# Staging the output sums of a four-pass MLP in contiguous scratch and reordering its seven block products

## The chip, the cores and the metric

The kernel runs on one core of a Trainium2 chip as one program. The metric is the device time of that program in microseconds (us); several executions are timed and their median is given. One execution is also recorded by the hardware profiler, and all rows below come from it. The engines are called PE (TensorE, matrix products; PEld is its weight load), ACT (ScalarE), DVE (VectorE), POOL (GpSimd) and SP (SyncE, which here only issues transfers). L1302 is line 1302 of the kernel file.

## What is computed

Three layers follow one another: an attention with random features, a mixture of experts in which each of 2304 tokens goes through one of 8 experts, and a dense MLP. The change touches the MLP alone:

```python
def _moe2_ref(x, w_in, w_out):          # x 2304x512, w_in 512x2048, w_out 2048x512
    h = x @ w_in
    g = np.where(h >= 1, h, np.where(h <= -1, 0.0, (h + 1) ** 2 / 4))
    return (g @ w_out).astype(np.float32)
```

Inside the kernel the tokens stand sorted by expert, so a finished row of the output has to be written to the row of its token.

## The kernel before, in words

Attention and experts end near 399 us of the trace; the MLP fills the rest. Every float32 factor is split in a high and a low part, and a product is three matrix products: high by high, high by low, low by high.

**Passes and groups.** The 2048 hidden columns are taken in four passes `qd` of 512 columns (four blocks `f` of 128). The 2304 tokens are six groups `g` of G = 384 (three tiles `t` of 128). For each pass and group a hidden step makes g, and an output step `z_o(qd, g, fs)` multiplies it with 512 rows of w_out: 36 matmuls of 512 columns, half of them for blocks 0 and 1, half for blocks 2 and 3, into three PSUM banks `po`, one for each tile. Each output is thus a sum over four passes.

**Output sums before.** After the second half of `z_o`, ACT copies each bank to a tile `tmp` of 512 columns (L1298), and `z_store` (L1302) lets POOL issue an indirect transfer that scatters the 128 rows to the output tensor in DRAM: a plain write in pass 0, an accumulating one in passes 1 to 3. That is 15 tiles times 4 passes. The last group's three tiles (`ends`) are summed on chip in `acc` and written once at the end.

**The ring `tmp`.** `temp()` (L1236) hands out four buffers in turn. Three users share them: these copies, the four block combinations of `y_sums` (pass 0), and the four temporaries of `s_h` (s1, u2, s5, u3). A buffer that fed a transfer comes free when the transfer has landed.

**Pass 0** uses plain products, `z_h` (24 matmuls of 384 columns for two blocks). In between, POOL forms sums of blocks of the input (`y_sums`, L1312), ACT and DVE split them, and SP writes them to scratch `yd` in DRAM.

**Passes 1 to 3** take pairs `p` of token groups and halves `a` of the hidden blocks by Strassen's scheme in Winograd's form: `s_h(qd, p, a)` needs seven products instead of eight. Each product is six matmuls of 384 columns. They go to four PSUM banks b1 to b4, and ACT and DVE add the banks up to four results q11, q12, q21, q22, each followed by `z_clip` and `z_g` (clip, square, maximum, split). Each `s_h` is followed by the output step of one group, so a pass is six half steps, each an `s_h` and a `z_o`. The seven factors of the tokens come from `yd` through a ring of nine slots `yS`/`ys`; POOL issues a load (`y_load`, L1329, 768 KB) each time a product with a = 1 has read its slot.

**Order on the engines.** Every engine works through its instructions in program order. Between the output step and the next `s_h` stand calls of `w_advance`, which turn raw weights into float32 (`w_float32`: ACT L248, DVE L249 to L252) and split them. For each pass, two of these calls end in `w_sums` (L308), which forms the block sums of the weights: copies on ACT (L290), sums and low parts on POOL (L317 to L323, L293). The sums for passes 2 and 3 stand right before `s_h(qd, 0, 1)` and `s_h(qd, 1, 1)` of passes 1 and 2; those for pass 1 stand in pass 0.

At the end of the program a branch looks whether any expert had more tokens than its place holds (here none), and then the three tiles of `acc` are stored.

Of the kernel before, what the change touches and what calls it, by code (L numbers as in the profile page):

```python
# [8 lines left out]
F32 = mybir.dt.float32  # L9
# [4 lines left out]
AF = mybir.ActivationFunctionType  # L14
# [5 lines left out]
P = 128  # L20
# [141 lines left out]
def kernel(  # L162
# [145 lines left out]
    def w_sums(qd, sub, a, b):  # L308
        if sub == 0:
            for i in range(7):  # L310
                w_new(("wi", qd, "A", i))
        a11, a21 = [a.rearrange("p (a i f) -> p i a f", a=2, i=2)[:, i] for i in range(2)]
        a12, a22 = [b.rearrange("p (a i f) -> p i a f", a=2, i=2)[:, i] for i in range(2)]
        w_op(qd, 0, sub, a11)
        w_op(qd, 2, sub, a22)
        s1, s2, s3, s4 = a22, a11, a21, a22
        nc.gpsimd.tensor_add(s1, a21, a22)  # L317
        nc.gpsimd.tensor_sub(s3, a11, a21)
        nc.gpsimd.tensor_sub(s2, s1, a11)
        w_op(qd, 1, sub, s2)  # L320
        w_op(qd, 3, sub, s1)
        w_op(qd, 4, sub, s3)
        nc.gpsimd.tensor_sub(s4, a12, s2)  # L323
        for i, t in ((5, a12), (6, s4)):
            if qd == 1:
                w_op(qd, i, sub, t)
            else:
                wlast.append((qd, i, sub, t))
# [907 lines left out]
    def temp():  # L1236
        return zp.tile([P, 512], F32, name="tmp", tag="tmp", bufs=4)

# [61 lines left out]

    def z_store(t, src, op=ALU.bypass):
        nc.gpsimd.indirect_dma_start(  # L1302
            out=outs[t], out_offset=bass.IndirectOffsetOnAxis(ap=oidx[:, t:t + 1], axis=0),
            in_=src, in_offset=None, compute_op=op)


    def y_keep(u):
        p, i = divmod(u, 2)
        for j, op in (((0, 0), (1, 5)) if i == 0 else ((1, 6),)):
            nc.sync.dma_start(out=yd[p][op], in_=ys[u % 2][:, j * 4 * G:j * 4 * G + 4 * G].bitcast(F32))  # L1310

    def y_sums(p, s):  # L1312
        b11, b12, b21, b22 = [yT[2 * i + s][:, (2 * p + j) * G:(2 * p + j) * G + G] for i in range(2) for j in range(2)]
        t1, t2, t3, t4 = [temp()[:, 0:G] for _ in range(4)]
# [4 lines left out]
        for i, (op, t) in enumerate(((3, t1), (4, t3), (1, t2), (2, t4))):  # L1319
            tag = "g0" if i % 2 else "g1"  # L1320
# [11 lines left out]
    def s_h(qd, p, a):  # L1332
        k0 = 7 * (3 * (qd - 1) + p)
        b1, b2, b4, b3 = [ps_h2.tile([P, 512], F32, name="ph2", tag="ph2")[:, 0:G] for _ in range(4)]

        def product(i, bank, first, final):
            y = yslots[(k0 + i) % NSL].rearrange("p (s h c) -> p s h c", s=2, h=2)
# [8 lines left out]

        s1, u2, s5, u3 = [temp()[:, 0:G] for _ in range(4)]
# [21 lines left out]
        q12 = z_clip(u2)  # L1369
        z_g(*q22, (qd, g1, f1), nc.vector)  # L1370
        z_g(*q12, (qd, g1, f0), nc.vector)


# [51 lines left out]
    tot = nc.values_load(ints[0:1, 3, 0:1], min_val=0, max_val=8 * 16)  # L1425
    yT = y_tiles("yF")
    fw = [yT[j // 10][:, j % 10 * 256:j % 10 * 256 + 256] for j in range(16)]
# [8 lines left out]
    with tc.If(tot > 0):  # L1436
        for t in ends:
            nc.sync.dma_start(out=sd[t * P:(t + 1) * P, :], in_=acc[t])
        nc.sync.dma_start(out=ld.rearrange("(t p) o -> p t o", p=P), in_=oidx.rearrange("p (t o) -> p t o", o=1))
        for e in range(E):  # L1440
# [4 lines left out]
            with tc.For_i(0, cnt_e, 1) as i:  # L1445
# [54 lines left out]
                nc.sync.dma_start(out=sd[bass.ds(c0, 128), :], in_=fo)  # L1500
        for t in ends:
            nc.sync.dma_start(out=acc[t], in_=sd[t * P:(t + 1) * P, :])
    for t in ends:
        z_store(t, acc[t])

# [30 lines left out]
```

## Time and profile before

| | us |
|---|---|
| median of 3 runs | 948.33 |
| lowest and highest | 945.34, 952.28 |
| the profiled execution | 952.49 |
| its span in the trace | 950.7 |
| PE busy in it | 794.0 |
| MLP, from the first to the last matmul | 399.4 to 938.5 |

A profiled row gives an instruction's start, its duration, engine, line and operands. Square brackets at its end give how long the engine had stood idle before it, and which instruction or transfer ended that idleness. The granted clock of TensorE is shown as a share of full speed.

### The profile page before, as it was taken

To read this page: it belongs to the slowest core of one execution; us is meant where nothing else is said; L and a number is where in the kernel's file an instruction comes from. 1 tells how busy PE (TensorE), PEld (TensorE's weight loads), DVE (VectorE), ACT (ScalarE), POOL (GpSimd) and SP (SyncE) were. 2 spreads that over 40 slices of the span, in tenths; PEclk is the share of its full clock that TensorE was granted. 3 is DMA by queue.
4 is the path that set the end of the run, shared out by engine and by line. 5 is a ranking of instruction groups with operands and counts; after the bars stand their busy time and mean duration, and the time that the engine had idled before them with its cause. 6 is when DMAs were issued, how large, how long until landed. Compare 5 with 4: busy or idle time off the path is not lost. (4 is left out here: it accounts for less than half of the span.)

```text
span 950.7 us, 17112 instructions
## 1 busy us (share of the span) xinstructions
PE 794.0 (84%) x6428; PEld 715.9 (75%) x6428; DVE 541.1 (57%) x1097; ACT 412.3 (43%) x999; POOL 500.7 (53%) x527
## 2 busy tenths in 40 slices
PE   6897996899999999966587885968877779898984
PEld 5786885699999999955466774858666668787873
DVE  4578788566668565773554545444464444553441
ACT  6897995333222222343444443333333333443340
POOL 5468814455554552666555736463546464564333
PEclk9999998899999999987889997979988989998998
DMA  9956112556676655452445765584927484854723
GB/s 221 236 125 175 36 36 90 159 177 198 203 214 195 198 181 171 157 182 89 176 155 189 269 262 211 126 267 100 299 55 272 94 276 73 243 216 75 208 33 70
DMA packets 97260, 159.53 MB, mean 168 GB/s; under 512 B 28864, under 2 KB 61760, under 8 KB 97168
## 3 DMA queue, kind: packets, MB, share of 16 engines
q1 hardware_dynamic: 77408, 84.47, 29.8%
q0 software_dynamic: 18864, 72.16, 25.8%
q10 hardware_dynamic: 896, 1.70, 0.5%
q8 instruction: 53, 0.87, 0.4%
q14 instruction: 39, 0.32, 0.1%
HBM read 120.57 MB, written 37.75 MB: 167 GB/s over the span
## 5 line engine op out<-in xcount | busy, mean ns | idle before, releaser
L1286 PE MATMUL po<-wh,g 128*128 128x512 f32 x288 | 120.8, 419 | 40.0 <-ACT g L1249 23.4
L1250 POOL TENSOR_TENSOR g<-cl,g 128x384 fp32r<-128x384 f32 x60 | 65.6, 1101 | 156.8 <-ACT g L1249 121.3
L272 POOL TENSOR_SCALAR wh<-wraw 128x1024 fp32r<-128x1024 f32 x60 | 74.2, 1238 | 102.4 <-DMA wraw<-in_moe_w_dram 60.8
L1288 PE MATMUL po<-wh,g 128*128 128x512 f32 x288 | 120.7, 419 | 3.2 <-POOL g L1250 3.1
L1302 POOL DMA_INDIRECT out_dram<-tmp,oidx x60 | 88.0, 1467 | 60.0 <-ACT tmp L1298 47.6
L1287 PE MATMUL po<-wl,g 128*128 128x512 f32 x288 | 119.1, 414 | 0.0
L1286 PEld LDWEIGHTS po<-wh,g 128*128 128x128 f32 x288 | 57.9, 201 | 55.2 <-ACT g L1249 26.0
L1242 ACT ACTIVATE cl<-cl,half 128x384 f32<-128x384 f32 x96 | 56.1, 612 | 91.7 <-DVE cl L1241 91.7
L340 DVE TENSOR_TENSOR wl<-wraw,wh 128x1024 fp32r<-128x1024 f32 x60 | 86.9, 1456 | 9.8 <-POOL wh L272 9.8
L570 ACT ACTIVATE pp<-ps,bi 128x128 f32<-128x128 f32 x288 | 84.5, 480 | 3.1 <-DVE bi L566 3.1
L1341 PE MATMUL ph<-yS,wh 128*128 128x384 f32 x140 | 52.0, 372 | 37.4 <-DVE tmp L1352 31.8
L1110 PE MATMUL ph<-xh,wh 128*128 128x288 f32 (+6 forms) x256 | 77.6, 303 | 2.7 <-DVE hl L1116 2.2
L1128 PE MATMUL py<-hh,wh 128*128 128x288 f32 (+6 forms) x256 | 77.5, 303 | 0.0
L1111 PE MATMUL ph<-xl,wh 128*128 128x288 f32 (+6 forms) x256 | 77.2, 302 | 0.1
L1112 PE MATMUL ph<-xh,wl 128*128 128x288 f32 (+6 forms) x256 | 77.1, 301 | 0.0
L1130 PE MATMUL py<-hh,wl 128*128 128x288 f32 (+6 forms) x256 | 76.4, 299 | 0.0
L1129 PE MATMUL py<-hl,wh 128*128 128x288 f32 (+6 forms) x256 | 76.3, 298 | 0.0
L1288 PEld LDWEIGHTS po<-wh,g 128*128 128x128 f32 x288 | 57.7, 200 | 23.0 <-POOL g L1250 9.5
L1249 ACT ACTIVATE g<-cl 128x384 fp32r<-128x384 f32 x96 | 50.2, 525 | 46.7 <-DVE cl L1248 43.5
L1341 PE MATMUL ph<-ys,wh 128*128 128x384 f32 x112 | 43.1, 385 | 30.0 <-DVE tmp L1352 27.7
L1287 PEld LDWEIGHTS po<-wl,g 128*128 128x128 f32 x288 | 57.9, 201 | 12.6
L293 POOL TENSOR_TENSOR wl<-wz,wh 128x256 fp32r<-128x256 f32 (+1 forms) x54 | 49.3, 1019 | 28.2 <-ACT wh L290 27.9
(208 smaller groups left out, 2096.4 us busy)
## 6 DMA issues: line engine op xcount, KB each, us to landing
wraw<-in_moe_w_dram SPq DMA_DIRECT2D x57, 512.0 KB, 4.0
yS<-yd POOLq DMA_DIRECT2D x35, 768.0 KB, 9.4
ys<-yd POOLq DMA_DIRECT2D x28, 768.0 KB, 9.0
yd<-g SPq DMA_DIRECT2D x24, 384.0 KB, 2.6
wraw<-in_moe_w_in_dram SPq DMA_DIRECT2D x16, 512.0 KB, 4.7
wraw<-in_moe_w_out_dram SPq DMA_DIRECT2D x16, 512.0 KB, 4.3
yd<-ys SPq DMA_DIRECT2D x9, 768.0 KB, 7.1
blk<-in_k_dram SPq DMA_DIRECT2D x8, 512.0 KB, 7.1
```

Of the source, the lines that this page charges most:

```text
L340: nc.vector.tensor_sub(lo, t, hi.bitcast(F32))
L570: act.activation(at(ppb)[:, 2 * j + i, :], at(pjb[i])[:, j, :], AF.Exp, bias=r["bi"][:, j, i:i + 1])
L1110: nc.tensor.matmul(ph, lhsT=wh[:, d, c], rhs=xh, start=(d == 0), stop=False)
L1111: nc.tensor.matmul(ph, lhsT=wh[:, d, c], rhs=xl, start=False, stop=False)
L1112: nc.tensor.matmul(ph, lhsT=wl[:, d, c], rhs=xh, start=False, stop=(d == 3))
L1128: nc.tensor.matmul(py, lhsT=wh[:, a, c], rhs=hh, start=(f == 0), stop=False)
L1130: nc.tensor.matmul(py, lhsT=wl[:, a, c], rhs=hh, start=False, stop=(f == 7))
L1286: nc.tensor.matmul(po, lhsT=gh[:, c], rhs=wh, start=(f == 0), stop=False)
L1287: nc.tensor.matmul(po, lhsT=gh[:, c], rhs=wl, start=False, stop=False)
L1288: nc.tensor.matmul(po, lhsT=gl[:, c], rhs=wh, start=False, stop=(f == 3))
L1302: nc.gpsimd.indirect_dma_start(out=outs[t], out_offset=bass.IndirectOffsetOnAxis(ap=oidx[:, t:t + 1], axis=0), in_=src, in_offset=None, co ...
L1341: nc.tensor.matmul(bank, lhsT=wh[:, s, :], rhs=y[:, s, 0, :], start=(first and s == 0), stop=False, **skip)
```

## The change

Scratch `zd` in DRAM holds the running sums of one group as one contiguous block, 128 partitions by 1536 columns (768 KB). Two staging tiles `sts` on chip take the three tiles of a group side by side. Passes 0 to 2 copy the three banks there with ACT; pass 0 then writes the block with one plain transfer on SP's queue, passes 1 and 2 with one accumulating transfer issued by POOL. In pass 3, SP fetches the block two groups ahead of its use, DVE adds the banks to it, and three plain indirect transfers scatter the finished rows. The last group is treated likewise, except that its rows are stored at the end. In pass 0 only one of the two staging tiles exists.

`temp()` becomes a ring of five buffers of 384 columns, which only `y_sums` and `s_h` use.

The seven products are renumbered and reordered. Product 2 now completes bank b1 (q11), right behind products 0 and 1; its clip and `z_g` move forward with it. `w_sums` and `y_sums` form the same blocks under the new numbers: three of the seven weight copies now need no sum and come first.

```diff
+    zd = [dram.tile([P, G // P * D], F32, name=f"zd{g}") for g in range(NT // G)]
...
         w_op(qd, 0, sub, a11)
-        w_op(qd, 2, sub, a22)
-        s1, s2, s3, s4 = a22, a11, a21, a22
+        w_op(qd, 3, sub, a22)
+        w_op(qd, 2, sub, a12)
+        s1, s2, s3, s4 = a21, a11, a22, a12
         nc.gpsimd.tensor_add(s1, a21, a22)
-        nc.gpsimd.tensor_sub(s3, a11, a21)
         nc.gpsimd.tensor_sub(s2, s1, a11)
         w_op(qd, 1, sub, s2)
-        w_op(qd, 3, sub, s1)
-        w_op(qd, 4, sub, s3)
+        w_op(qd, 4, sub, s1)
+        nc.gpsimd.tensor_sub(s3, a22, s2)
         nc.gpsimd.tensor_sub(s4, a12, s2)
-        for i, t in ((5, a12), (6, s4)):
+        for i, t in ((5, s3), (6, s4)):
...
+        sts[0] = flat[:, 1024:1024 + TG * D]
     ends = range(NTILE - TG, NTILE)
-    acc = {t: zp.tile([P, D], F32, name=f"acc{t}", tag=f"acc{t}", bufs=1) for t in ends}
+    sts = [None, zp.tile([P, TG * D], F32, name="st1", tag="st1", bufs=1)]
...
-        return zp.tile([P, 512], F32, name="tmp", tag="tmp", bufs=4)
+        return zp.tile([P, G], F32, name="tmp", tag="tmp", bufs=5)
...
-            if t in ends:
-                if qd == 0:
-                    nc.scalar.activation(acc[t], po, AF.Copy)
-                else:
-                    nc.vector.tensor_add(acc[t], acc[t], po)
+            st = z_stage(qd, g)[:, j * D:j * D + D]
+            if qd < 3:
+                nc.scalar.activation(st, po, AF.Copy)
             else:
-                st = temp()
-                nc.scalar.activation(st, po, AF.Copy)
-                z_store(t, st, ALU.add if qd else ALU.bypass)
+                nc.vector.tensor_add(st, st, po)
+                if t not in ends:
+                    z_store(t, st)
+        if fs[0] == 0:
+            return
+        if qd == 0:
+            nc.sync.dma_start(out=zd[g], in_=z_stage(qd, g))
+        elif qd < 3:
+            nc.gpsimd.dma_start(out=zd[g], in_=z_stage(qd, g), accum_op=ALU.add)
+        elif g + 2 < NG:
+            z_fetch(g + 2)
+
+    def z_stage(qd, g):
+        return sts[g % 2 if qd else 1]
+
+    def z_fetch(g):
+        nc.sync.dma_start(out=z_stage(3, g), in_=zd[g])
...
-        product(0, b1, True, False)
+        product(0, b1, True)
         nc.scalar.activation(s1, b1, AF.Copy)
-        product(1, b2, True, False)
+        product(1, b2, True)
         nc.vector.tensor_add(u2, b2, s1)
-        product(2, b4, True, True)
-        product(3, b3, True, False)
+        product(2, b1, False)
+        q11 = z_clip(b1)
+        product(3, b4, True)
+        z_g(*q11, (qd, g0, f0), nc.gpsimd)
+        product(4, b3, True)
         nc.scalar.activation(s5, b3, AF.Copy)
-        product(4, b2, False, True)
+        product(5, b2, False)
         nc.vector.tensor_add(u3, b2, s1)
         c21 = s1
         nc.vector.tensor_sub(c21, u3, b4)
         q21 = z_clip(c21)
         nc.vector.tensor_add(s5, u3, s5)
+        q22 = z_clip(s5)
         z_g(*q21, (qd, g0, f1), nc.gpsimd)
-        product(5, b1, False, True)
-        q11 = z_clip(b1)
-        q22 = z_clip(s5)
-        z_g(*q11, (qd, g0, f0), nc.gpsimd)
-        product(6, b3, False, True)
+        product(6, b3, False)
...
     for qd in range(1, 4):
+        if qd == 3:
+            z_fetch(0)
...
             if p == 0:
                 w_finish(True)
+                if qd == 3:
+                    z_fetch(1)
```

Three places show what moves. The first is POOL in pass 0, from the last split of one group to the combinations of `y_sums` (L1315 to L1318 before, L1328 to L1331 after); `out_dram` is the output tensor. Before:

```order
L1250 TENSOR_TENSOR g_6708<-cl,g_6708 128x384
L1250 TENSOR_TENSOR g_6712<-cl,g_6712 128x384
L1302 DMA out_dram<-tmp,oidx 2304x512 x3
L1315 TENSOR_TENSOR tmp<-yT 128x384
L1316 TENSOR_TENSOR tmp<-yT_3140,yT 128x384
L1317 TENSOR_TENSOR tmp<-yT_3140,tmp 128x384
L1318 TENSOR_TENSOR tmp<-tmp,yT_3140 128x384
```

and now:

```order
L1252 TENSOR_TENSOR g_6701<-cl,g_6701 128x384
L1328 TENSOR_TENSOR tmp<-yT 128x384
L1329 TENSOR_TENSOR tmp<-yT_3146,yT 128x384
L1330 TENSOR_TENSOR tmp<-yT_3146,tmp 128x384
L1331 TENSOR_TENSOR tmp<-tmp,yT_3146 128x384
```

The three scattering transfers between the split and the combinations are gone from POOL; one plain transfer stands on SP's queue instead.

The second place is ACT in one half step of pass 1 (third `s_h`), from the copies of the output banks on; the numbers tell buffers apart, and `wx` is the weight conversion. Before:

```order
L1298 ACTIVATE tmp_7245<-po_7218 128x512
L1298 ACTIVATE tmp_7254<-po_7219 128x512
L1298 ACTIVATE tmp_7263<-po_7220 128x512
L248 ACTIVATE wx_7268<-wraw_7096 128x512
L1350 ACTIVATE tmp_7278<-ph2_7274 128x384
L1355 ACTIVATE tmp_7280<-ph2_7277 128x384
L1242 ACTIVATE cl_7317<-cl_7317,half_104 128x384
L1249 ACTIVATE g0_7321<-cl_7317 128x384
```

and now:

```order
L1295 ACTIVATE yW_6792<-po_7198 128x512
L1295 ACTIVATE yW_6792<-po_7199 128x512
L1295 ACTIVATE yW_6792<-po_7200 128x512
L249 ACTIVATE wx_7243<-wraw_7076 128x512
L1363 ACTIVATE tmp_7253<-ph2_7249 128x384
L1244 ACTIVATE cl_7277<-cl_7277,half_110 128x384
L1251 ACTIVATE g0_7286<-cl_7277 128x384
L1371 ACTIVATE tmp_7255<-ph2_7252 128x384
```

The output copies no longer take buffers of `tmp`, and the square and the rounding of q11 stand ahead of the copy s5.

The third place is POOL before the weight sums of `s_h(1, 1, 1)`. Before:

```order
L1302 DMA out_0_dram<-tmp_7386,oidx_102 2304x512
L1302 DMA out_0_dram<-tmp_7395,oidx_102 2304x512
L1302 DMA out_0_dram<-tmp_7404,oidx_102 2304x512
L293 TENSOR_TENSOR wl1_109<-wz2_5922,wh1_108 128x256
L293 TENSOR_TENSOR wl2_111<-wz3_5923,wh2_110 128x256
L317 TENSOR_TENSOR wz3_5923<-wz2_5922,wz3_5923 128x2x128
L318 TENSOR_TENSOR wz2_5922<-wz2_5922 128x2x128
L319 TENSOR_TENSOR wz2_5922<-wz3_5923,wz2_5922 128x2x128
```

and now:

```order
L1305 DMA zd1_69<-st1_5930 128x1536
L294 TENSOR_TENSOR wl1_115<-wz2_5928,wh1_114 128x256
L294 TENSOR_TENSOR wl3_119<-wz3_5929,wh3_118 128x256
L294 TENSOR_TENSOR wl2_117<-wz3_5929,wh2_116 128x256
L319 TENSOR_TENSOR wz2_5928<-wz2_5928,wz3_5929 128x2x128
L320 TENSOR_TENSOR wz2_5928<-wz2_5928 128x2x128
```

One transfer stands where three stood, and five POOL instructions lead to the second sum, as before.

## Rows read from the trace of the kernel before

**Rows 1.** Waits from 399.4 us on: who waited for whom, us, times, longest.
```profile
ACT tmp L1355 <- DMA out_dram<-tmp,oidx: 70.2, 13, 8.5
...
PE ph L1341 <- DVE tmp L1352: 59.5, 14, 11.5
```
**Rows 2.** Windows by pass: length, busy us (instructions) of PE, PEld, DVE, ACT, POOL; clock, DMA share, GB/s.
```profile
399.40:548.50 149.10, 110.08 (x489) 93.00 (x488) 82.13 (x122) 66.19 (x133) 90.91 (x95) 0.89 0.52 185
548.50:684.00 135.50, 102.24 (x451) 90.51 (x450) 64.90 (x113) 49.85 (x97) 65.17 (x72) 0.87 0.66 211
684.00:819.40 135.40, 106.40 (x469) 93.03 (x468) 67.56 (x117) 51.23 (x101) 72.64 (x75) 0.87 0.60 175
819.40:938.60 119.20, 109.83 (x505) 95.64 (x503) 52.85 (x98) 44.54 (x85) 54.28 (x49) 0.94 0.52 123
```
**Rows 3.** The same view by half step, six of them.
```profile
565.90:594.90 29.00, 17.53 (x79) 15.66 (x78) 14.91 (x24) 12.86 (x26) 17.75 (x22) 0.82 0.51 183
...
614.70:642.00 27.30, 18.32 (x80) 16.37 (x79) 12.11 (x22) 9.92 (x21) 19.64 (x22) 0.81 0.78 242
...
704.90:731.70 26.80, 17.47 (x80) 15.54 (x79) 15.94 (x24) 9.99 (x21) 18.28 (x23) 0.81 0.54 194
...
751.80:778.80 27.00, 17.97 (x79) 16.02 (x78) 12.04 (x21) 9.70 (x20) 19.54 (x22) 0.81 0.73 221
...
836.30:852.00 15.70, 15.70 (x79) 14.01 (x78) 9.91 (x19) 7.87 (x16) 11.45 (x14) 1.00 0.63 233
...
893.60:909.40 15.80, 15.80 (x80) 14.20 (x79) 7.49 (x14) 5.69 (x11) 5.24 (x4) 1.00 0.39 51
```
**Rows 4.** Timeline of the half step at 893.6: starts of products 1 and 2, ACT's copy s1.
```profile
894.69 0.33 PE L1341 MATMUL ph<-yS,wh 128*128 128x384 f32 x1
894.89 0.49 ACT L1350 ACTIVATE tmp<-ph 128x384 f32<-128x384 f32 x1 [0.47 <-PE ph L1343]
...
895.73 0.33 PE L1341 MATMUL ph<-yS,wh 128*128 128x384 f32 x1
```
**Rows 5.** Timeline of the half step at 565.9, weight sums: ACT, then PE.
```profile
579.66 1.03 ACT L290 ACTIVATE wh<-wz 128x256 fp32r<-128x256 f32 x3 [3.24 <-POOL wz L319]
580.59 0.47 ACT L1350 ACTIVATE tmp<-ph 128x384 f32<-128x384 f32 x1
...
581.71 0.69 PE L1341 MATMUL ph<-yS,wh 128*128 128x384 f32 x1 [11.47 <-DVE tmp L1352]
```
**Rows 6.** Timeline of the half step at 614.7, weight sums: POOL, ACT, PE.
```profile
618.55 1.56 POOL L1302 DMA_INDIRECT out_dram<-tmp,oidx  x1 [0.30 <-issue]
...
623.98 1.03 ACT L290 ACTIVATE wh<-wz 128x256 fp32r<-128x256 f32 x3 [5.99 <-POOL wz L319]
...
625.47 0.47 ACT L1350 ACTIVATE tmp<-ph 128x384 f32<-128x384 f32 x1
...
628.09 0.69 PE L1341 MATMUL ph<-yS,wh 128*128 128x384 f32 x1 [8.98 <-DVE tmp L1352]
```
**Rows 7.** Timeline of pass 0, fourth group: POOL, then PE.
```profile
500.97 0.99 POOL L1302 DMA_INDIRECT out_dram<-tmp,oidx  x1 [0.15 <-issue]
...
504.53 1.03 POOL L1315 TENSOR_TENSOR tmp<-yT 128x384 f32<-128x384 f32 x1
...
513.23 0.50 PE L1286 MATMUL po<-wh,g 128*128 128x512 f32 x1 [4.76 <-ACT g L1249]
```
**Rows 8.** POOL's groups of instructions, 545 to 951 us: busy us, mean ns, idle before.
```profile
L1302 POOL DMA_INDIRECT out_dram<-tmp,oidx x47 | 75.1, 1597 | 56.8 <-ACT tmp L1298 47.4 <-issue 6.4 <-ACT tmp L1350 1.2
...
L1329 POOL DMA_DIRECT2D yS<-yd x30 | 18.5, 661 | 0.9 <-PE ph L1343 0.9
```
**Rows 9.** Transfers, whole span: issues, KB each, median us from issue to landing.
```profile
yS<-yd POOLq DMA_DIRECT2D x35, 768.0 KB, 9.4
```
**Rows 10.** The same view, 440 to 545 us (plain writes).
```profile
out_dram<-tmp,oidx POOLq DMA_INDIRECT x14, 2.7
```
**Rows 11.** The same view, 545 to 660 us (accumulating writes).
```profile
out_dram<-tmp,oidx POOLq DMA_INDIRECT x11, 7.8
```

More of the change, by code (lines that the diff above doesn't have):

```diff
@@ L1290, in z_o, with z_store @@
                 continue
-            if t in ends:
-                if qd == 0:
-                    nc.scalar.activation(acc[t], po, AF.Copy)
-                else:
-                    nc.vector.tensor_add(acc[t], acc[t], po)
-            else:
-                st = temp()
-                nc.scalar.activation(st, po, AF.Copy)
-                z_store(t, st, ALU.add if qd else ALU.bypass)
-    def z_store(t, src, op=ALU.bypass):
+            st = z_stage(qd, g)[:, j * D:j * D + D]
+            if qd < 3:
+                nc.scalar.activation(st, po, AF.Copy)
+            else:
+                nc.vector.tensor_add(st, st, po)
[13 more added lines that the diff above has]
+        nc.sync.dma_start(out=z_stage(3, g), in_=zd[g])
+    def z_store(t, src):
         nc.gpsimd.indirect_dma_start(
             out=outs[t], out_offset=bass.IndirectOffsetOnAxis(ap=oidx[:, t:t + 1], axis=0),
-            in_=src, in_offset=None, compute_op=op)
+            in_=src, in_offset=None)
     def y_keep(u):
         p, i = divmod(u, 2)
-        for j, op in (((0, 0), (1, 5)) if i == 0 else ((1, 6),)):
+        for j, op in (((0, 0), (1, 2)) if i == 0 else ((1, 6),)):
             nc.sync.dma_start(out=yd[p][op], in_=ys[u % 2][:, j * 4 * G:j * 4 * G + 4 * G].bitcast(F32))
@@ L1313, in y_sums @@
         b11, b12, b21, b22 = [yT[2 * i + s][:, (2 * p + j) * G:(2 * p + j) * G + G] for i in range(2) for j in range(2)]
-        t1, t2, t3, t4 = [temp()[:, 0:G] for _ in range(4)]
+        t1, t2, t3, t4 = [temp() for _ in range(4)]
         nc.gpsimd.tensor_sub(t1, b12, b11)
@@ L1318, in y_sums @@
         nc.gpsimd.tensor_sub(t4, t2, b21)
-        for i, (op, t) in enumerate(((3, t1), (4, t3), (1, t2), (2, t4))):
+        for i, (op, t) in enumerate(((4, t1), (5, t3), (1, t2), (3, t4))):
             tag = "g0" if i % 2 else "g1"
@@ L1334, in s_h, with product @@
         b1, b2, b4, b3 = [ps_h2.tile([P, 512], F32, name="ph2", tag="ph2")[:, 0:G] for _ in range(4)]
-        def product(i, bank, first, final):
+        def product(i, bank, first):
             y = yslots[(k0 + i) % NSL].rearrange("p (s h c) -> p s h c", s=2, h=2)
@@ L1345, in product @@
                 y_load(k0 + NSL + i)
-        s1, u2, s5, u3 = [temp()[:, 0:G] for _ in range(4)]
+        s1, u2, s5, u3 = [temp() for _ in range(4)]
         f0, f1, g0, g1 = 2 * a, 2 * a + 1, 2 * p, 2 * p + 1
-        product(0, b1, True, False)
+        product(0, b1, True)
         nc.scalar.activation(s1, b1, AF.Copy)
-        product(1, b2, True, False)
+        product(1, b2, True)
         nc.vector.tensor_add(u2, b2, s1)
-        product(2, b4, True, True)
-        product(3, b3, True, False)
+        product(2, b1, False)
[3 more added lines that the diff above has]
+        product(4, b3, True)
         nc.scalar.activation(s5, b3, AF.Copy)
-        product(4, b2, False, True)
+        product(5, b2, False)
         nc.vector.tensor_add(u3, b2, s1)
@@ L1361, in s_h @@
         nc.vector.tensor_add(s5, u3, s5)
+        q22 = z_clip(s5)
         z_g(*q21, (qd, g0, f1), nc.gpsimd)
-        product(5, b1, False, True)
-        q11 = z_clip(b1)
-        q22 = z_clip(s5)
-        z_g(*q11, (qd, g0, f0), nc.gpsimd)
-        product(6, b3, False, True)
+        product(6, b3, False)
         nc.vector.tensor_add(u2, u2, b3)
-        q12 = z_clip(u2)
         z_g(*q22, (qd, g1, f1), nc.vector)
-        z_g(*q12, (qd, g1, f0), nc.vector)
+        z_g(*z_clip(u2), (qd, g1, f0), nc.vector)
     for u in range(NG):
@@ L1425 @@
     tot = nc.values_load(ints[0:1, 3, 0:1], min_val=0, max_val=8 * 16)
-    yT = y_tiles("yF")
+    flat = yp.tile([P, 3 * YW], F32, name="yF", tag="yT")
+    yT = [flat[:, d * YW:(d + 1) * YW] for d in range(3)]
+    yT.append(zp.tile([P, 8 * G], F32, name="yF3", tag="ys1", bufs=1))
+    last = z_stage(3, NG - 1)
     fw = [yT[j // 10][:, j % 10 * 256:j % 10 * 256 + 256] for j in range(16)]
@@ L1436 @@
     with tc.If(tot > 0):
-        for t in ends:
-            nc.sync.dma_start(out=sd[t * P:(t + 1) * P, :], in_=acc[t])
+        for j, t in enumerate(ends):
+            nc.sync.dma_start(out=sd[t * P:(t + 1) * P, :], in_=last[:, j * D:j * D + D])
         nc.sync.dma_start(out=ld.rearrange("(t p) o -> p t o", p=P), in_=oidx.rearrange("p (t o) -> p t o", o=1))
@@ L1500 @@
                 nc.sync.dma_start(out=sd[bass.ds(c0, 128), :], in_=fo)
[L1501 to L1504, printed above, removed]
+        for j, t in enumerate(ends):
+            nc.sync.dma_start(out=last[:, j * D:j * D + D], in_=sd[t * P:(t + 1) * P, :])
+    for j, t in enumerate(ends):
+        z_store(t, last[:, j * D:j * D + D])
 _INS = ['q', 'k', 'v', 'omega', 'moe_w_gate', 'moe_w1', 'moe_w2', 'moe2_w_in', 'moe2_w_out']
```

## The prediction

> **What bounds the kernel now.** I read the windows by pass first, then the waits, then single half steps in the timeline.
>
> The MLP takes 539 us, and PE is busy for 428 of them at a granted clock of 0.87 to 0.94 [rows 2]. So PE sets the pace, but it stands idle for a fifth of the time and runs below full speed for part of the rest. What it could do is seen in the half steps at 836.3 and 893.6: 15.7 and 15.8 us, PE busy throughout, clock 1.00 [rows 3]. That is seven products at 1.05 us each (product 2 starts 1.04 us after product 1 [rows 4]) and 36 matmuls of `z_o` in the other 8.4 us. I take 15.75 us as the price of an unhindered half step and count everything above it as loss.
>
> Pass 1 (548.5 to 684.0) has six half steps, the first with only half of a `z_o`: 6 x 15.75 - 4.2 = 90.3 us unhindered, 135.5 measured, 45.2 lost. Pass 2: 94.5 against 135.4, 40.9 lost. Pass 3 has a `z_o` more at its end: 102.9 against 119.2, 16.3 lost. Together 102.4 us [rows 2].
>
> Two causes share this. Four half steps are 26.8 to 29.0 us long [rows 3]; they lose 110.1 - 63.0 = 47.1 us. In them PE waits about 9 to 11 us before product 4, nominally for DVE's u2; but u2 waits for ACT's copy s1, and s1 stands in ACT's queue behind the weight copies, which wait for POOL's sums [rows 5, 6]. This is the weight chain, not the ring `tmp`. The other 55.3 us are spread over the other half steps. There ACT's copy s5 waits for a transfer to the output to land, 70.2 us in 13 cases, because it needs a buffer of `tmp` that feeds that transfer [rows 1]. An accumulating one needs 7.8 us to land, a plain one needed 2.7 [rows 10, 11]. The two good half steps are those in which such a wait did not reach PE.
>
> In pass 0 PE's waits are the ends of chains through ACT, DVE and POOL. POOL issues three scattering transfers, from 500.97 to 504.53, and only then starts the sums of `y_sums`; behind these come the splits, the clips and, at the end, the first matmul of the next `z_o`, after 4.76 us idle [rows 7].
>
> **The change part by part.**
>
> *The ring `tmp`.* With the output copies out of it, no buffer of `tmp` feeds a transfer any more, so the waits of rows 1 on a landing disappear, and with them the main source of the 55.3 us. What is late next: I leave 12 us in place. 6 of them stay in the first half step (548.5 to 565.9 us: 17.4 us against 11.55), which follows the first loads of the y slots. The other 6 us are an estimate of 0.35 us for each of the other 17 half steps, for the new tightness described below. Gain 43.3 us.
>
> *Product order.* Product 2 now accumulates into b1, so it must wait until ACT has copied s1. Unhindered, s1 starts at 894.89 and ends at 895.38, and product 2 starts at 895.73 [rows 4]: 0.35 us to spare, where before there were three products. Any instruction of more than 0.35 us in front of s1 on ACT now shows on PE at once. In return u2 has three products to cover it instead of two.
>
> *The four weight chains stay,* since the number of steps to the second sum is the same; one copy less stands before s1 (three took 1.03 us [rows 5], so 0.34 us). In the half step at 565.9, s1 would end near 580.59 - 0.34 + 0.47 = 580.72, and PE resumes there instead of at 581.71: about 0.95 us earlier, but with five products left instead of three (2.1 us). Loss 1.15 us each time, twice (565.9 and 704.9). At 614.7 the chain also stands behind scattering issues on POOL: the last starts at 618.55, and ACT waits 5.99 us for the sums where it waits 3.24 in the other case [rows 5, 6]. That difference of 2.75 us goes. s1 then ends near 625.47 - 2.75 - 0.34 + 0.47 = 622.85, and PE resumes there rather than at 628.09, since u2's late DVE start no longer decides: 5.2 earlier, 2.1 more to do, gain 3.1 us, twice. All four: gain 3.9 us. If the new issue on POOL is as long as the three old ones, 2 x 2.75 us of it fail.
>
> *Transfers.* POOL loses 45 scattering issues in passes 0 to 2 (60 before, 15 of them in pass 3 which remain, plain now) and gains 12 accumulating ones. The trace has no direct accumulating transfer. Its issue lies between 0.66 us, a plain direct one, and 3 x 1.60 = 4.8 us, three accumulating scatters [rows 8]; I take 0.66 as the nearest form. It stands behind the half step's work on POOL and, apart from the weight chain, nobody waits there. Its landing lies between 9.4 us, a plain load of the same 768 KB [rows 9], and three accumulating scatters one after another, 23.4 us, behind such a load: 32.8 us [rows 9, 11]; I take 12. Two staging tiles alternate, so a tile is needed again by the first copy of the second next group, 2 x 15.75 - 8.4 + 2.8 = 25.9 us after its issue. At 12 us nothing waits; at 32.8 ACT waits 6.9 us.
>
> The Trainium skill ("DMA: Bandwidth & Descriptors", section "Anatomy of one DMA — SWDGE (gpsimd) path") gives 2.0 us plus bytes over 436 GB/s; by it, as an estimate, the block would land in 3.8 us. Its estimate for 256 KB, 2.6 us, agrees with the plain 2.7, but not with the accumulating 7.8 [rows 10, 11]; so the page is no lower end here.
>
> *Pass 3.* The fetch waits for the scatters of its tile (three issues at POOL, 2.7 us landing) and takes about 9.4 us [rows 9, 10]: some 17 us after the `z_o`, needed 25.9 us after it. For the last group two `z_o` follow each other and only 7.4 + 8.4 + 2.8 = 18.6 us are there; I charge 2 us at the end. Eighteen DVE additions replace ACT copies (nine additions in `acc` go); DVE is busy for 52.9 of 119.2 us in this pass [rows 2], which hides them; if they stood alone they would delay u2 in each half step.
>
> *Pass 0.* POOL's 3.56 us of issues before `y_sums` go [rows 7], in four groups. In two of them the chain leads on through the weights to the wait that stops PE, in two it ends directly in a wait of PE like the 4.76 us of rows 7. Gain 14 us, a little less than 4 x 3.56. The plain write moves to SP's queue, behind weight loads and ahead of the stores of `y_sums`; only one staging tile exists here, but it is needed again a whole group later. No cost.
>
> *Sum:* 43.3 + 3.9 + 14 - 2 = 59.2 us. 952.5 - 59.2 = 893.3 for the profiled execution; that one lay 0.44% above the median of the runs shown (952.49 against 948.33), so 889 us is forecast.
>
> **Rivals.**
>
> *Transfers become the bound (16%).* DMA engines are busy 0.52 to 0.66 of the passes [rows 2]: 89 us in pass 1, which would then last about 120. The average fits, but the loads come in bursts, seven per pair, and the new fetches add to them. A slot is reloaded about 17 us before its use; if landing doubles from 9.4 to 19 us, product 2 of each of nine pairs comes about 2 us late, and each stop costs another 1.8 us at the lower clock (PE busy 17.5 instead of 15.75 us in a stopped half step [rows 3]). 9 x 3.8 = 34 us given back: 927, or 923 at the median. The Trainium skill ("DMA: Bandwidth & Descriptors", section "Issuing engines are not separate DMA queues") speaks for it: SP's new transfers run on the same engines, so moving them saves only issue time. By that rule the forecast stands only as long as rows 2's share leaves room, which it does on average.
>
> *The copies become the bound (6%).* The 0.35 us of slack is gone if ACT's queue is usually late by 1.3 us, for example with q11's work ahead of s5. Then PE stops in 18 half steps for 1 us, plus 1.8 us of clock: 50 us given back, 943, or 939. Against it: in rows 4 ACT was idle for 0.47 us before s1.
>
> *Slower: the accumulating block lands too late (5%).* Place: the first output copy of each group in passes 1 and 2, on ACT, ahead of s1. It begins to cost at 25.9 us of landing and outweighs the 59.2 us, over six pairs, from 25.9 + 59.2 / 6 = 35.8 us on. At 40 us: 6 x 14.1 = 85 us, 978 in all, or 974. For it: an accumulating scatter lands three times as slowly as a plain one. Against: even my upper bound, 32.8 us, leaves a gain.
>
> *More than forecast (11%).* All half steps without weight sums reach 15.75 us, and the fetch is in time: 14 us and some clock more, 870 at the median.
>
> **How the numbers follow.** Forecast 62%, the others as given. About 1% is what a measurement of this kernel can tell from no change. Faster: forecast, bunched transfers and the better case, 0.89. Within 1%: the copies as the bound, 0.06. Slower: 0.05. The range takes in the better case and the bunched transfers with 2 us beyond: 866 to 925.
>
> **What would show it.** Right: no wait on a transfer into the output or `zd` in front of s1, s5, u2 or u3; half steps without weight sums below 17 us; four stops before product 2, instead of 4, in the weight half steps, 12.7 us long where it was 11.47 and near 6 us where it was 8.98 [rows 5, 6]; pass 0 near 135 us, passes 1 to 3 near 120, 116 and 107. Wrong: output copies on ACT that wait for `zd`; PE waiting for y slots; PE stopped before product 2 in most half steps; pass 0 no shorter.

## The result and the profile after

| | before | after |
|---|---|---|
| median of 4 runs, us | 948.38 | 879.26 |
| lowest and highest | 945.34, 952.28 | 876.56, 882.72 |
| the profiled execution | 952.49 | 878.48 |
| its span | 950.7 | 876.6 |
| MLP, first to last matmul | 399.4 to 938.5 | 393.2 to 868.4 |
| POOL busy in the span | 500.7 | 438.7 |

The ratio is 0.9271 with a 95% interval of 0.9223 to 0.9319: 69 us faster. The forecast was 889, with a range of 866 to 925.

The same view of windows by pass as in [rows 2], of the kernel after (length, busy us and instructions of PE, PEld, DVE, ACT and POOL, granted clock, DMA share, GB/s):

```profile
393.20:525.40 132.20, 105.26 (x489) 91.35 (x488) 81.64 (x121) 66.42 (x133) 77.50 (x81) 0.90 0.58 210
525.40:642.10 116.70, 95.34 (x451) 84.92 (x450) 62.02 (x114) 50.22 (x97) 47.17 (x62) 0.91 0.71 232
642.10:762.80 120.70, 99.63 (x469) 88.39 (x469) 66.40 (x114) 53.20 (x104) 50.66 (x65) 0.90 0.67 207
762.80:868.40 105.60, 103.77 (x505) 90.96 (x503) 58.59 (x109) 37.89 (x73) 43.66 (x49) 1.00 0.61 206
```

Against [rows 2], pass 0 is 16.9 us shorter, and passes 1 to 3 together 47.1 (343.0 against 390.1). In pass 3 PE is busy for 103.8 of 105.6 us, at full clock: that stage is done. Passes 1 and 2 still lose, and the half steps show where (as in [rows 3]):

```profile
539.80:570.60 30.80, 17.66 (x79) 15.74 (x79) 14.74 (x24) 13.15 (x27) 16.28 (x21) 0.78 0.66 234
586.20:610.60 24.40, 18.22 (x79) 16.36 (x78) 12.26 (x21) 9.86 (x20) 13.96 (x19) 0.86 0.79 255
660.20:692.00 31.80, 18.66 (x79) 16.77 (x78) 14.86 (x21) 12.16 (x24) 18.03 (x23) 0.73 0.69 221
707.70:731.30 23.60, 17.43 (x80) 15.44 (x79) 12.26 (x21) 9.87 (x20) 13.98 (x19) 0.86 0.80 262
610.60:626.40 15.80, 15.80 (x80) 14.09 (x80) 9.09 (x18) 7.48 (x14) 3.04 (x3) 1.00 0.56 155
```

The first four are the half steps with weight sums. The fifth stands for the twelve full ones without, which now last 15.7 to 18.0 us. The waits from 399 us on, as in [rows 1] (who waited for whom, us, times, longest):

```profile
PE ph L1354 <- ACT tmp L1363: 41.1, 7, 13.1
...
POOL zd L1305 <- ACT st L1295: 34.5, 6, 6.5
POOL zd L1305 <- ACT yW L1295: 30.8, 6, 5.2
...
PE ph L1354 <- DMA ys<-yd: 1.5, 2, 0.9
...
PE ph L1354 <- DMA yS<-yd: 0.5, 1, 0.5
```

No wait on a landing of the output or of `zd` is left. The kernel before had 155.3 us of them: the 70.2 of [rows 1] for ACT's copy s5, and two more rows of the same view, for DVE's u2 and u3:

```profile
DVE tmp L1352 <- DMA out_dram<-tmp,oidx: 47.5, 12, 8.4
...
DVE tmp L1357 <- DMA out_dram<-tmp,oidx: 37.6, 9, 6.0
```

PE waits 2.0 us in all for slots of y. What it waits for now in passes 1 to 3 is ACT's copy s1 (L1363), seven times, of which four waits are 13.14, 6.18, 13.14 and 6.17 us. POOL's waits are those of the accumulating transfer for the copies that fill its block; no engine is listed as waiting for this transfer.

Two of these four stops in the timeline, first the one that answers to [rows 5] (ACT, then PE), then the one that answers to [rows 6] (POOL, ACT, PE):

```profile
553.88 0.72 ACT L291 ACTIVATE wh<-wz 128x256 fp32r<-128x256 f32 x2 [2.69 <-POOL wz L320]
554.51 0.47 ACT L1363 ACTIVATE tmp<-ph 128x384 f32<-128x384 f32 x1
...
555.03 0.69 PE L1354 MATMUL ph<-yS,wh 128*128 128x384 f32 x1 [13.14 <-ACT tmp L1363]
...
587.29 0.88 POOL L1305 DMA_DIRECT2D zd<-st  x1 [5.61 <-ACT st L1295]
...
592.92 0.72 ACT L291 ACTIVATE wh<-wz 128x256 fp32r<-128x256 f32 x2 [2.69 <-POOL wz L320]
...
594.63 0.69 PE L1354 MATMUL ph<-yS,wh 128*128 128x384 f32 x1 [6.18 <-ACT tmp L1363]
```

ACT waits 2.69 us for the sums in both cases, where it waited 3.24 and 5.99. Pass 0, the place of [rows 7]: POOL goes from the splits straight into `y_sums`, and PE's wait at the end of that chain is 0.42 us where it was 4.76:

```profile
484.15 1.97 POOL L1252 TENSOR_TENSOR g<-cl,g 128x384 fp32r<-128x384 f32 x2 [4.17 <-ACT g L1251]
486.08 1.01 POOL L1328 TENSOR_TENSOR tmp<-yT 128x384 f32<-128x384 f32 x1
...
494.20 0.50 PE L1288 MATMUL po<-wh,g 128*128 128x512 f32 x1 [0.42 <-ACT g L1251]
```

POOL's transfers by group (busy us, mean ns of one), against [rows 8]:

```profile
L1316 POOL DMA_INDIRECT out_dram<-yW,oidx x9 | 8.9, 986 | 13.6 <-DVE yW L1297 12.0 <-issue 1.2 <-DVE tmp L1365 0.3
...
L1305 POOL DMA_DIRECT2D zd<-yW x6 | 5.4, 900 | 30.8 <-ACT yW L1295 30.8
```

And the transfers that are new on SP, with the median from issue to landing (against [rows 9 to 11]):

```profile
zd<-st SPq DMA_DIRECT2D x6, 768.0 KB, 3.6
...
yW<-zd SPq DMA_DIRECT2D x3, 768.0 KB, 4.2
st<-zd SPq DMA_DIRECT2D x3, 768.0 KB, 6.9
```

### The profile page after: what moved, and what is told of

The parts are those of the page before. It is cut to its first block, busy times and chain, and to the rows that moved or that the text cites. A ratio compares the mean times of both kernels' runs of the same rounds, so it can differ in the third digit from the quotient of the medians.

```text
span 876.6 us, 17032 instructions
## 1 busy us (share of the span) xinstructions
PE 766.4 (87%) x6428; PEld 696.3 (79%) x6428; DVE 542.0 (62%) x1106; ACT 407.9 (47%) x990; POOL 438.7 (50%) x494
## 4 chain that ended last, share of the span: by engine, by line
PE 62%; DVE 12%; ACT 11%; POOL 9%; issue 3%; DMA 2%; POOLq 0%; DVEq 0%; SPq 0%; ACTq 0%
PE po L1290 6%; PE po L1288 6%; PE po L1289 6%; PE ph L1354 5%; PE ph L1355 4%; PE ph L1356 4%; PE ph L1111 4%; PE py L1129 4%; PE py L1131 4%; PE ph L1112 4%; PE py L1130 4%; PE ph L1113 4%; ACT pp L571 4%; DVE wy L251 2%; ACT wh L291 2%
## 5 line engine op out<-in xcount | busy, mean ns | idle before, releaser
L1288 PE MATMUL po<-wh,g 128*128 128x512 f32 x288 | 116.7, 405 | 26.0 <-ACT st L1295 17.4
L1244 ACT ACTIVATE cl<-cl,half 128x384 f32<-128x384 f32 x96 | 58.1, 616 | 127.5 <-DVE cl L1243 125.2
L1290 PE MATMUL po<-wh,g 128*128 128x512 f32 x288 | 116.4, 404 | 1.0 <-POOL g L1252 1.0
L1289 PE MATMUL po<-wl,g 128*128 128x512 f32 x288 | 115.7, 402 | 0.0
L341 DVE TENSOR_TENSOR wl<-wraw,wh 128x1024 fp32r<-128x1024 f32 x60 | 84.8, 1422 | 6.3 <-POOL wh L273 6.3
L1288 PEld LDWEIGHTS po<-wh,g 128*128 128x128 f32 x288 | 55.7, 194 | 39.1 <-ACT st L1295 18.4
L1354 PE MATMUL ph<-yS,wh 128*128 128x384 f32 x140 | 50.1, 358 | 27.0 <-ACT tmp L1363 25.5
L1290 PEld LDWEIGHTS po<-wh,g 128*128 128x128 f32 x288 | 55.4, 192 | 16.7 <-POOL g L1252 3.8
L251 DVE SCALAR_TENSOR_TENSOR wy<-wx,wy 128x512 int32<-128x512 int32 x32 | 32.8, 1025 | 53.8 <-ACT wx L249 53.0
L1289 PEld LDWEIGHTS po<-wl,g 128*128 128x128 f32 x288 | 55.8, 194 | 12.0
L1116 ACT ACTIVATE hh<-ph 128x288 fp32r<-128x288 f32 (+6 forms) x64 | 26.8, 418 | 69.7 <-PE ph L1113 68.6
```

Source lines behind the costliest of these rows:

```text
L341: nc.vector.tensor_sub(lo, t, hi.bitcast(F32))
L1354: nc.tensor.matmul(bank, lhsT=wh[:, s, :], rhs=y[:, s, 0, :], start=(first and s == 0), stop=False, **skip)
```

## Experiments

The theory: passes 1 to 3 gain by the ring alone, because no buffer of `tmp` feeds a transfer any more; pass 0 gains by POOL's issues; the order of products is worth little; and what remains is s1 behind the weight chain. The rivals: the contiguous block itself (fewer, larger transfers) or the order makes the gain, and what remains is something else.

**The ring alone (e1_ring).** The kernel before, with its scattering transfers and its order, but with output copies in buffers of their own and `tmp` as five buffers of 384 columns instead of four of 512:

```diff
-        return zp.tile([P, 512], F32, name="tmp", tag="tmp", bufs=4)
+        return zp.tile([P, G], F32, name="tmp", tag="tmp", bufs=5)
...
-                st = temp()
+                st = so[j] if qd else acc[ends[j]]
```

> The kernel before, with one thing changed: the output copies get buffers of their own (in passes 1 to 3 three in the spare columns of yW, in pass 0 the three tiles of acc), and tmp, now five buffers of 384 columns, serves only the block combinations. Scattering accumulating transfers, product order and weight order stay as before. Theory A (the gain of passes 1 to 3 is the end of the waits for a landing in tmp): the half steps without weight sums fall to about 15.8 us, the four with weight sums stay at 27 to 29 us, pass 0 stays near 149 us; 898 to 912 us in all. Theory B (the product order carries the gain): the waits only move to other copies and the time stays above 930 us.

Measured: 901.53 us, ratio 0.9509 (0.9461 to 0.9557). Its windows, pass 0 and passes 1 to 3:

```profile
395.00:543.70 148.70, 114.31 (x487) 95.99 (x486) 82.34 (x122) 66.15 (x133) 91.39 (x95) 0.85 0.52 187
543.70:886.80 343.10, 300.25 (x1423) 265.89 (x1421) 186.49 (x327) 145.72 (x283) 191.85 (x195) 0.94 0.67 194
```

Passes 1 to 3 take 343.1 us with 45 scattering issues still in them, and 343.0 in the kernel after. No wait on a landing of the output is left here either. So the ring alone gives as much as these passes gained; scratch and order add nothing there on balance. In parts they do differ: in the kernel after, the first half step of pass 1 is 5.3 us shorter than here (14.3 against 19.5), while the four half steps with weight sums are 3.8 us longer together (110.7 against 106.9). What the fifth buffer is worth beside the separation was not tried by itself. Pass 0 stays at 148.7, where before had 149.1: its gain comes from elsewhere.

**The order alone (e2_order).** The kernel before, with the new order of products, weight terms and `y_sums`:

```diff
-        product(2, b4, True, True)
-        product(3, b3, True, False)
+        product(2, b1, False)
+        q11 = z_clip(b1)
+        product(3, b4, True)
+        z_g(*q11, (qd, g0, f0), nc.gpsimd)
+        product(4, b3, True)
```

> The kernel before with the new product order alone (w_sums, y_sums and s_h as in the changed kernel); tmp, its four buffers of 512 columns, and the scattering transfers stay. Theory A: the waits for a landing stay in front of s5 and u2, so no gain: 938 to 962 us. Theory B: the half steps without weight sums get shorter by 3 us and more each, 915 us or less.

Measured: 937.65 us, ratio 0.9921 (0.9887 to 0.9955): 8.6 us faster than the kernel before, a small gain whose interval does not reach 1 (the expectation began at 938). Of the waits on landings, those of u2 (L1352) and u3 (L1360) on DVE remain, 66.1 us where before had 85.1; s5's on ACT, 70.2 us before, are almost gone (third row):

```profile
DVE tmp L1352 <- DMA out_dram<-tmp,oidx: 41.4, 11, 7.1
...
DVE tmp L1360 <- DMA out_dram<-tmp,oidx: 24.7, 9, 4.6
...
ACT tmp L1358 <- DMA out_dram<-tmp,oidx: 2.9, 2, 1.8
```

**The change without the order (e3_old_order).** The kernel after, with the order of before:

```diff
-        product(2, b1, False)
...
+        product(2, b4, True, True)
...
+        product(5, b1, False, True)
```

> The changed kernel with the product order and the weight order of before; scratch, staging and the ring of five stay. Theory A: half steps without weight sums at 15.8 us as in the changed kernel; in the four with weight sums PE stops before product 4 again, with three products left, so these are 1 to 2 us shorter in the first pair of a pass; 872 to 884 us. Theory B: 905 us or more.

Measured: 878.98 us, ratio 0.9290 (0.9249 to 0.9331), the same as after. The stops stand before product 4 again and are 12.00, 6.74, 12.22 and 6.77 us (first row); in exchange the small stops before product 2 are gone. Passes 1 to 3 last 341.0 us (second row):

```profile
557.68 0.69 PE L1354 MATMUL ph<-yS,wh 128*128 128x384 f32 x1 [12.00 <-DVE tmp L1365]
...
526.00:867.00 341.00, 300.25 (x1424) 267.01 (x1422) 193.57 (x336) 141.04 (x274) 144.47 (x177) 0.93 0.67 217
```

**When the block lands (e4_one_stage).** The kernel after with a single staging tile in passes 1 and 2, so that the next group's first copy needs it less than one half step after the issue:

```diff
-        return sts[g % 2 if qd else 1]
+        return sts[g % 2 if qd == 3 else 1]
```

> The changed kernel with one staging tile instead of two in passes 1 and 2, so that an output copy waits for the accumulating transfer of the group just before, about 10 us after its issue. This measures the landing, which the trace does not give. If the block lands within 10 us (as fast as a plain one): 876 to 884 us, no wait of the copies. If it lands in about 12 us: waits of some 2 us in up to 11 groups, most of them hidden because the banks are needed only a half step later, 880 to 900 us. If it lands like three accumulating scatters one after another (23 us and more): 950 us or more.

Measured: 882.19 us, ratio 0.9305 (0.9266 to 0.9344), not told apart from after. No copy of these two passes waits for `zd`. Two rows of its timeline: the issue, and ACT's next copy into the same tile, which waits for nothing (no idle time in brackets):

```profile
576.94 0.94 POOL L1305 DMA_DIRECT2D zd<-st  x1 [5.15 <-ACT st L1295]
...
589.45 0.58 ACT L1295 ACTIVATE st<-po 128x512 f32<-128x512 f32 x1
```

So it had landed within 12.5 us. The DMA line from 575 to 605 us, 40 slices of 0.75 us, narrows it: all DMA engines fall silent after the fourteenth slice in GB/s, at 575 + 14 x 0.75 = 585.5 us, so the block had been moved 8.6 us after the issue began (the line shows the moving itself, not when its end is signalled):

```profile
DMA  9991978999792000000000000968989880000798
GB/s 401 426 385 49 131 82 139 202 205 238 246 407 98 22 0 0 0 0 0 0 0 0 0 0 0 131 115 172 229 180 238 306 366 11 0 0 0 175 382 290
```

**POOL's issue time in pass 0 (e5_pool3).** The kernel after, with the block of pass 0 written by POOL in three direct transfers:

```diff
-            nc.sync.dma_start(out=zd[g], in_=z_stage(qd, g))
+            for j in range(TG):
+                nc.gpsimd.dma_start(out=zd[g][:, j * D:j * D + D], in_=z_stage(qd, g)[:, j * D:j * D + D])
```

> The changed kernel, but pass 0 writes each group with three transfers issued by POOL in front of the sums of y_sums, as many as before the change, though plain and contiguous, instead of one on SP's queue. If POOL's time for these issues is what pass 0 had lost: it gets longer by about three issues of 0.7 to 0.9 us in four or five groups, 8 to 13 us, and the whole lies at 887 to 893 us. If it was something else (the ring, the scattered rows): no more than 3 us, 877 to 882 us.

Measured: 887.80 us, ratio 0.9374 (0.9322 to 0.9426). Pass 0 by window, and the group of the new issues:

```profile
393.60:532.50 138.90, 109.53 (x488) 93.51 (x487) 82.58 (x122) 66.41 (x133) 83.69 (x95) 0.88 0.55 199
...
L1304 POOL DMA_DIRECT2D zd<-st x18 | 9.9, 561 | 3.3 <-ACT st L1295 3.3
```

Three issues of 0.561 us are 1.68 us; in the four groups with `y_sums` behind them that is 6.7 us, and pass 0 is 138.9 - 132.2 = 6.7 us longer (8 to 13 were expected, from issues of 0.7 to 0.9 us). What POOL issues ahead of `y_sums` is paid in full here. The scattering issues of before were longer (0.99 us in [rows 7]); whether scattering costs pass 0 anything beyond that is not shown.

**What remains, in three cuts.** The weight stage (`w_advance`: conversion and splits, then `w_sums`) stands between a `z_o` and s1 in ACT's queue. First the sums alone are put behind the `s_h` (e6_defer_sums), then whole stages (e7_weights_after), then stages behind this `s_h` and sums behind the next one (e8_both):

```diff
# e6_defer_sums, after the w_advance calls
             s_h(qd, p, 1)
+            while wsums:
+                w_sums(*wsums.pop(0))
# e7_weights_after: the calls of w_advance moved
+            s_h(qd, p, 1)
             if qd < 3:
                 for _ in range((2, 2, 1)[p]):
                     w_advance()
-            s_h(qd, p, 1)
```

> The changed kernel, with the weight sums of passes 2 and 3 formed right behind s_h(qd, p, 1) instead of in front of it; the conversion of the weights stays in front. If the four stops of PE come from ACT's copy s1 behind the chain of these sums: in the first pair s1 starts about 7 us after the half step instead of 15, in the second 3 to 5 instead of 8; the half step after each gets some 2 us longer; 12 to 24 us less in all, 855 to 867 us. If something else holds s1 back (the conversion, DVE): 876 us or more.

> The changed kernel, with the conversion of the weights and their sums, all of what stood in front of s_h(qd, p, 1), moved behind it. The chain then runs on ACT beside the output step and stands in front of the output copies and of s1 of the next half step. If the chain's length on ACT decides, its 11 us start about 5 us earlier against PE: stops of 3 to 8 us in front of product 2 of the following half step instead of 13 and 6 in this one; 860 to 872 us. If PE's stops only move: 876 to 884 us.

> The changed kernel, with the conversion moved behind s_h(qd, p, 1) and the sums moved further, behind s_h of the next pair, so that the chain is cut in two pieces of 4 to 6 us, each beside another output step. If the length of what stands in front of s1 decides: stops of at most 3 us in each place; 845 to 862 us. If PE's stops only move: 876 us or more.

Measured: e6_defer_sums 873.39 us, ratio 0.9225 (0.9184 to 0.9266), which misses its expectation; e7_weights_after 874.89, ratio 0.9242 (0.9199 to 0.9284), which lies between the two ranges of its expectation; e8_both 859.36, ratio 0.9054 (0.8995 to 0.9113). Some of e8_both's deferred sums are formed from tiles that the next conversion had already overwritten, so it computes with other weights; each engine runs as many instructions as in the kernel after. In e6_defer_sums the stops of 13.1 and 6.2 us become 6.0 and 0.9, but the sums now stand before s1 of the next half step and stop PE for 2.9 and 2.7 us there. In e7_weights_after much of the first stop follows the stage into the next half step:

```profile
572.56 0.69 PE L1354 MATMUL ph<-yS,wh 128*128 128x384 f32 x1 [7.60 <-ACT tmp L1363]
```

Only cut in two, so that no single half step has both in front of its s1, does the chain mostly fit beside PE's work.

**The chain cut in two (e9_two_pieces), and the same with the old order (e10_two_pieces_old).** e9_two_pieces forms the sums behind the first `s_h` of the next pair, and a later stage writes to their tiles only after that; e10_two_pieces_old adds the old order of products, weight terms and `y_sums`:

```diff
             s_h(qd, p, 0)
...
+            while wsums:
+                w_sums(*wsums.pop(0))
+            if p and qd < 3:
+                w_advance()
...
+            s_h(qd, p, 1)
             if qd < 3:
                 for _ in range((2, 2, 1)[p]):
                     w_advance()
-            s_h(qd, p, 1)
...
-            if qd < 3:
+            if p == 2 and qd < 3:
                 w_advance()
```

> The changed kernel, with a stage of weights (splits and w_block) started behind s_h(qd,p,1) and its sums formed at the head of the next pair, so that neither stands in front of s1 in the queue of ACT while the other does. If what stands in front of s1 in the weight half steps is what the changed kernel still loses (47.7 us over four half steps), the stops there fall from 13.1 and 6.2 us to 4 us or less and the time to 850 to 866 us, faster than the changed kernel by at least 12 us. If the loss only moves to the half steps that follow, or comes back as lower granted clock, it stays at 874 or above.

> The same with the old order of products, weight terms and y sums. If the order of products has a worth that the long weight chain hid in the comparison of the changed kernel with the old order (878.98 against 879.26), it shows here: product 2 no longer needs s1, so there is slack where the new order has 0.35 us, and the old order comes out 3 us or more faster; if u2 before product 4 is the tighter place, 3 us or more slower. If the order is worth nothing, the two agree within 2 us.

Measured: e9_two_pieces 858.89 us, ratio 0.9077 (0.9023 to 0.9131), and e10_two_pieces_old 850.02 us, ratio 0.8972 (0.8934 to 0.9010): both beat both kernels, and the intervals of the two do not meet. Passes 1 to 3 of e9_two_pieces and PE's waits in them:

```profile
524.70:846.60 321.90, 298.52 (x1422) 263.01 (x1421) 181.90 (x336) 138.72 (x274) 144.02 (x177) 0.97 0.70 230
...
PE ph L1358 <- ACT tmp L1367: 20.5, 13, 3.3
```

The same of e10_two_pieces_old:

```profile
529.00:844.20 315.20, 298.57 (x1423) 265.25 (x1421) 189.85 (x336) 139.49 (x274) 145.61 (x177) 0.96 0.71 234
...
PE ph L1358 <- DVE tmp L1369: 13.8, 5, 3.8
```

With the same work, the new order stops PE 13 times for s1 and the old one 5 times for u2; passes 1 to 3 differ by 6.7 us. Four of the stops, of 2.9 to 3.8 us, stand in the same half steps in both (12.9 and 13.4 us together); the other nine of the new order are 2.1 us or less each and 7.6 together, the other one of the old is 0.4. In the comparison of after with e3_old_order this did not show. The likely reason is that four long stops decided there, and they are about as long in either order (38.6 us together in after, 37.7 in e3_old_order).

## Why the prediction was right, step by step

The mechanism held and the total came out, but that passes 1 to 3 gained 47.0 us where 47.2 were forecast (by pass 116.7, 120.7 and 105.6 us, where 120, 116 and 107 were named) is luck: two terms were off by some 4.5 us in opposite directions. The terms for the profiled executions, us gained:

| term | predicted | measured |
|---|---|---|
| ring: half steps without weight sums | 43.3 | 47.7 |
| the four weight chains | 3.9 | -0.7 |
| pass 0 | 14 | 16.9 |
| the end, from the last matmul on | -2 | 4.0 |
| before the MLP (code unchanged) | 0 | 6.2 |
| sum | 59.2 | 74.1 |

*The ring.* Right in its cause, as e1_ring shows; one reading on the way to it was not. The prediction puts the loss on s5's waits for a landing and takes it that they are what reaches PE. In the half steps without weight sums, PE's stops end ten times on u2 (20.7 us) and only twice on s5 (5.6 us). One of them in the kernel before (DVE's u2, PE's product 4, ACT's s5):

```profile
600.96 0.56 DVE L1352 TENSOR_TENSOR tmp<-ph,tmp 128x384 f32<-128x384 f32 x1 [3.23 <-DMA out_dram<-tmp,oidx]
...
601.57 0.44 PE L1341 MATMUL ph<-yS,wh 128*128 128x384 f32 x1 [2.29 <-DVE tmp L1352]
...
602.22 0.49 ACT L1355 ACTIVATE tmp<-ph 128x384 f32<-128x384 f32 x1 [5.55 <-DMA out_dram<-tmp,oidx]
```

u2 had waited for the landing; PE went on as soon as u2 was formed, before s5's copy began. The three copies draw on the same ring, so the term did not suffer. What stays in these half steps is 7.6 us, not 12: 2.7 in the first, behind the y loads (6 were left for it), 2.3 in the one at 642.1, 2.3 in the first two of pass 3, and 0.3 in the rest. The one at 642.1 stops for 0.73 us before product 2 and for 1.03 before product 6, for s5; the two of pass 3 stop for 0.73 and 1.03 us before product 2. The 0.35 us of slack for s1 was read correctly, and its price here was small. The forecast charged it for 17 half steps, four of which are the weight half steps that have their own term. Ten of the twelve full half steps are below the 17 us that were named as a sign; those at 642.1 (18.0) and at 779.6 (17.04) are not.

*The weight chains.* Here a term failed. The stops moved before product 2 as stated, and their lengths (13.14 and 6.18 us) are close to the 12.7 and 6 of the forecast. Both half steps of p = 1 came out at 24.46 and 23.57 us where 27.2 - 3.1 = 24.1 followed. The first of p = 0 is 30.85 instead of 29.04 + 1.15 = 30.2. The second is 31.85 instead of 26.78 + 1.15 = 27.9, and this 3.9 us is most of the term's error of 4.6. The step that failed is "loss 1.15 us each time, twice": it took the half step at 704.9 to be like that at 565.9. It wasn't. At 704.9 the last group's sums were made by DVE in `acc` (first row below, timeline of the kernel before; then DVE's step of the weight conversion and ACT's); after, ACT copies them into the stage, and ACT's `wx`, which DVE waits for, starts 2.8 us into the half step instead of 0.5:

```profile
703.97 1.88 DVE L1295 TENSOR_TENSOR acc<-acc,po 128x512 f32<-128x512 f32 x3
...
707.01 1.60 DVE L250 SCALAR_TENSOR_TENSOR wy<-wx,wy 128x512 int32<-128x512 int32 x1
...
705.45 0.66 ACT L248 ACTIVATE wx<-wraw 128x512 f32<-128x512 f32 x1
```

The same place after (ACT, POOL, DVE):

```profile
660.37 0.60 ACT L1295 ACTIVATE st<-po 128x512 f32<-128x512 f32 x1 [0.80 <-PE po L1290]
...
662.95 0.65 ACT L249 ACTIVATE wx<-wraw 128x512 f32<-128x512 f32 x1
...
664.36 2.74 POOL L294 TENSOR_TENSOR wl<-yW,wh 128x512 fp32r<-128x512 f32 x2
...
663.63 4.02 DVE L251 SCALAR_TENSOR_TENSOR wy<-wx,wy 128x512 int32<-128x512 int32 x1 [5.44 <-ACT wx L249]
```

Besides starting later, DVE's step takes 4.02 us where it took 1.60. The prediction counted the additions that leave DVE, but not the three copies that ACT takes on in that half step.

*Pass 0.* Right: 135 was forecast, 132.2 measured, and e5_pool3 shows that issues on POOL cost what they last, in four groups. The four times 3.56 us make 14.2 of the 16.9; the rest is not assigned. That all of the 14.2 was gained follows from e5_pool3 by analogy, since no run takes the scattering issues away and nothing else.

*The transfers.* Landing of the accumulating block was taken as 12 us, with bounds of 9.4 to 32.8; in e4_one_stage it was moved in 8.6, which is under the lower bound. The rival "lands too late", which begins to cost at 25.9 us, falls with e4_one_stage, where half that time was enough. The issue on POOL is 0.88 to 0.93 us, not 0.66, and no engine is listed as waiting for it. The fetch lands in 4.2 to 6.9 us instead of 9.4, and no instruction waits for it: the 2 us charged at the end were not due. Besides, the last scatters start 0.2 us after the last addition, where 2.7 us lay between them before; this was not foreseen, and not pursued.

*The rivals.* "Transfers become the bound": the DMA share rose from 0.66 to 0.71 in pass 1 [rows 2], and still PE waited only 2.0 us for slots in all; e9_two_pieces and e10_two_pieces_old run at 0.70 and 0.71 over all three passes, with 2.8 and 2.2 us of such waits. "The copies become the bound": not in after, where s1 was late by 0.7 to 1.0 us in three of the half steps without weight sums; but once the weight chain is cut, late copies s1 account for most of what separates e9_two_pieces from e10_two_pieces_old, 6.7 us rather than 50.

*Before the MLP.* The 6.2 us there are no part of the change: e2_order, with the buffers of before, begins the MLP at 392.6 us, e1_ring at 395.0, e10_two_pieces_old at 396.3. So this start varies by some us with the same code ahead of it, and the profiled execution of before began late. It accounts for the two profiled executions differing by 74.0 us and the medians by only 69.1.

## What to carry to other kernels

A ring of temporaries that also feeds transfers makes every user wait for landings: separate those users first, for here buffers alone gave 45 of the 69 us. A shorter queue is worth what stands behind it, no more: POOL's added issues in pass 0 were paid in full, while 45 scattering issues in passes 1 to 3 cost nothing on balance. And compare an order of work once the longest wait is out of the way: the new order looked neutral until the weight chain was cut, and was then 1% slower.

## What was not expected of the hardware

DVE's step L251 (two inputs of 512 columns in SBUF, the on-chip memory) took 4.02 us once and 0.69 to 1.52 elsewhere in the MLP. It began at 663.63 and ended at 667.65, 0.55 us after the last of the four POOL instructions that were running since 661.89. It took 4.0 us at this same place in e3_old_order, e4_one_stage, e5_pool3 and e6_defer_sums too (e5_pool3 has a second long one of 3.14), and in the kernel before and the other six runs none took longer than 1.6. The Trainium skill ("SBUF — State Buffer", section "SBUF: two separate sides") describes a pair of ports that DVE, with two inputs in SBUF, and a POOL instruction that reads SBUF can't hold at once: whichever starts first has it for its whole instruction, and the other is blocked. The rows agree in that DVE's step did not end before POOL's run did. But the step at 544.67, beside a POOL run of three such instructions (543.13 to 547.30), took only 1.50 us, and that of before at 707.01, beside the same four (704.06 to 709.76), took 1.60, so the rule alone doesn't say when it happens.

An accumulating transfer of 768 KB in one contiguous block was moved in at most 8.6 us by e4_one_stage's DMA line, about as long as the 7.8 us to landing of an indirect one of 256 KB [rows 11]; and the plain indirect issues of pass 3 take 0.97 to 0.99 us of POOL where the accumulating ones of [rows 8] took 1.60.
